# First half-blocks of an attention and FFN kernel: three exponentials for a pair of heads instead of four, and four instructions in another place

## The chip, the cores and the metric

The kernel runs on one core of a Trainium2 chip. Five engines work side by side, each through its own instruction list in order: TensorE (PE in the profile, its weight loads PEld), VectorE (DVE), ScalarE (ACT), GpSimd (POOL) and SyncE (SP). They wait for each other by semaphores only. Transfers from and to HBM are issued from the queues of POOL, SP and ACT and carried by 16 DMA engines. TensorE writes into PSUM, eight banks of 128 partitions x 2 KB; VectorE and ScalarE read PSUM, POOL does not.

The metric is the device time of one execution in microseconds, the median of several runs.

## The reference

Inputs are q, k, v of shape (4, 8, 768, 64) in float32 (batch, heads, sequence, head size) and the weights of an FFN of 512 to 2048 to 512. An attention in which each query sees only the six best chunks of 32 keys is followed by an FFN with a squared relu.

```python
k_min, k_max = k_chunks.min(3), k_chunks.max(3)          # (B, H, 24, 64)
ub = sum(maximum(q * k_min, q * k_max), -1)              # upper bound per query and chunk
ub = where(causal, ub, -1e9)
top_chunks = argsort(ub)[..., -6:]
scores = q @ k.T / 8
scores = where(selected_chunk & causal, scores, -1e9)
attn = softmax(scores)
x = (attn @ v) as (B * S, H * D)                         # (3072, 512)
h = maximum(x @ w_in, 0)
out = (h * h) @ w_out
```

## The kernel before

The work is cut into half-blocks of 384 queries (three tiles of 128): `ORDER` lists (batch, half) as (0,0), (1,0), (0,1), (1,1), (2,0) and so on. Each half-block has four slots, one for each pair of heads; slot s of the first group (s = 0 to 3, `s < NP`) is pair s of batch 0, half 0. The order of instructions is written out by hand: a loop over the first four slots, then a loop over the others, in which FFN steps of earlier half-blocks are put between attention steps from a `queue`.

Steps of a slot, by name and line:

- `step_T` (L267, L274): TensorE transposes the packed keys and queries of a slot into PSUM. In the first loop, keys of slot s+2 go to the pool psF (two banks, shared with FFN blocks), queries to psY (one bank).
- `relus_T` (L295, ScalarE): relu of the queries and of their negative, for the bounds.
- `extrema` (L237, L240, VectorE): minimum and maximum of each chunk of keys, and their block form. Parts 0, 1 and 2 can be placed apart.
- `place` (L300): copies transposed keys or queries to where the scores read them, one copy for each head; by ScalarE or VectorE, as the call says.
- `step_U` (L378, L382, L396, L398): bounds of all chunks by TensorE, the eight largest by VectorE, and a compare that marks the chunks not selected.
- `step_V` (L431, L436 in the first group; L442, L447 later): transposes the marks (in the first group with the queries) and copies them next to the queries. The scores of the slot need this copy. The marks enter the scores as 32 more rows of the contraction.
- `step_E(s, hh, n)` (L460, L468, L471): scores of head hh for PSUM bank n, and their exponential by ScalarE into `e`. In a half 0, a head has six causal blocks of 128x128: `BANKS[0]` puts four of them (keys of tiles 0 and 2) into a first bank of 512 columns, and two (keys of tile 1) into columns 256 to 511 of a second one. In the first group the causal triangle is added in PSUM by one more matmul for each diagonal block (L468, `tri`); from slot 4 on POOL zeroes it after the exponential (L475).
- `step_F` (L493, L502, L503): probabilities times v, division by the sum, into `x`.
- `x_T`, `x_copy` (L531, L537): for the first half-block, x is transposed by TensorE in two parts (pairs 0 and 1, pairs 2 and 3), and copied out of PSUM as one [128x768] copy each.
- `ffn_up` (L579, L585, L589, L590): one of 16 blocks of the hidden layer, with relu on ScalarE and square on VectorE; `ffn_down` (L602): a quarter of an output tile. `push(0)` queues the first half-block's FFN in slot 4.

The end of slot 3 leads over to slot 4: x's first part is copied by ScalarE, then ScalarE places slot 4's queries and half of its keys, and in slot 4 (`if s == NP`) slot 5 is transposed, x's second part copied by VectorE, slot 4's head 0 computed and slot 5's queries placed by ScalarE.

In slot s of the first loop the order is: head 0's first bank, keys of s+2 transposed, head 0's second bank, head 1's first bank, bounds of s+1, three filler matmuls (`busy`), head 1's second bank, queries of s+2 transposed, marks of s+1 transposed, `step_F(s-1)`.

Loads are issued by POOL from lists by slot (`at(s, ...)`, `go`). The FFN's first matrix comes in three transfers (512, 512 and 1024 of its 2048 columns), the second in two. Each POOL transfer uses one of eight semaphores in turn, so an issue waits until the transfer eight before it has landed.

Of the kernel before, what the change touches and what calls it, by code (L numbers as in the profile page):

```python
# [8 lines left out]
F32 = mybir.dt.float32  # L9
BF16 = mybir.dt.bfloat16  # L10
AX = mybir.AxisListType
ALU = mybir.AluOpType
ACT = mybir.ActivationFunctionType
# [9 lines left out]
BANKS = (  # L23
# [3 lines left out]
)  # L27
# [12 lines left out]
def kernel(  # L40
# [9 lines left out]
    nc = tc.nc  # L50
# [3 lines left out]
    NP = H // 2  # L54
# [4 lines left out]
    scale = 1.0 / (D ** 0.5)  # L59

    consts = ctx.enter_context(tc.tile_pool(name="consts", bufs=1))
    work = ctx.enter_context(tc.tile_pool(name="work", bufs=2))
    psS = ctx.enter_context(tc.tile_pool(name="psS", bufs=3, space=bass.MemoryType.PSUM))
# [8 lines left out]
    KR = D + CR  # L72

    kqs = [consts.tile([128, NP, 4, 2, HB], BF16, tag=f"kq{i}", name="kq") for i in range(2)]
# [75 lines left out]
    ident = consts.tile([128, 128], BF16, tag="ident")  # L150
    make_identity(nc, ident)

    tri = consts.tile([128, 128], BF16, tag="tri", name="tri")
# [64 lines left out]
    def col_of(half, j, i):  # L218
        for n, bank in enumerate(BANKS[half]):
            for (at, jj, i0, m) in bank:  # L220
                if jj == j and i0 <= i < i0 + m:
                    return 512 * n + at + 128 * (i - i0)
        raise KeyError

    slots = [(b, half, p) for b, half in ORDER for p in range(NP)]
    NS = len(slots)
    st = {}
# [16 lines left out]
    def in_order(x):  # L244

        return x.rearrange("r (j p) -> r p j", j=TP)

    def by_token(x):
        return x.rearrange("r (p j) -> r p j", j=TP)
# [36 lines left out]
    def relus_T(s):  # L286
        b, half, p = slots[s]
        t = st[s]
        qr = t["qr"] = work.tile([128, 2, HB], BF16, tag="qr", bufs=3, name="qr")
        c = 128 * (1 - half)  # L290
        for w in range(2):
            o, i = qr[:, w, c:], t["q"][:, c:]
            if s >= NP:
                o, i = by_token(o), in_order(t["q"])[:, c // TP:, :]
            nc.scalar.activation(o, i, ACT.Relu, scale=(-1.0, 1.0)[w])  # L295

    def place(s, n, copy, h0=0, h1=2):
        b, half, p = slots[s]
        for h in range(h0, h1):
            copy(by_token(kqs[b % 2][0:D, p, 2 * half + "kq".index(n), h, :]),  # L300
                 in_order(st[s][n][D * h:D * h + D]))
# [103 lines left out]
    def qc(s, h):  # L405
        b, half, p = slots[s]
        return kqs[b % 2][0:KR, p, 2 * half + 1, h, :]
# [16 lines left out]
    def step_V(s):  # L424
# [21 lines left out]
        for h in range(2):  # L446
            nc.vector.tensor_copy(  # L447
                kqs[b % 2][D:KR, p, 2 * half + 1, h, c:], qt[CR * h:CR * h + CR, c:])

    def step_E(s, hh, n):  # L450
        b, half, p = slots[s]
        t = st[s]
        if n == 0:
            t["e"][hh] = work.tile([128, 1920], BF16, tag="e", bufs=4, name="e")
        e = t["e"][hh]
        ps = psS.tile([128, 512], F32, tag="ps", name="ps")
        lo, hi = 512, 0
        for (at, j, i0, m) in BANKS[half][n]:
            c = 128 * (i0 - HT * half)
            nc.tensor.matmul(  # L460
                ps[:, at:at + 128 * m],
                lhsT=kqs[b % 2][0:KR, p, 2 * (j // HT), hh,
                                128 * (j % HT):128 * (j % HT + 1)],
                rhs=qc(s, hh)[:, c:c + 128 * m], start=s >= NP or lo == 512, stop=s >= NP)
            lo, hi = min(lo, at), max(hi, at + 128 * m)
        if s < NP:
            for (at, j, i0, m) in BANKS[half][n]:
                nc.tensor.matmul(  # L468
                    ps[:, at:at + 128], lhsT=ident, rhs=tri, start=False,
                    stop=at == BANKS[half][n][-1][0])  # L470
        nc.scalar.activation(e[:, 512 * n + lo:512 * n + hi], ps[:, lo:hi], ACT.Exp,  # L471
                             scale=float(scale))
        if n == 1 and s >= NP:
            d = e[:, 0:1152].rearrange("p (a c) -> p a c", a=3)[:, :, 0:128]
            nc.gpsimd.affine_select(  # L475
                out=d, in_=d, compare_op=ALU.is_ge, fill=0.0, base=0,
                channel_multiplier=-1, pattern=[[0, 3], [1, 128]])
# [5 lines left out]
    def step_F(s, hh):  # L483
        b, half, p = slots[s]
        t = st[s]
        if hh == 0:
            t["po"] = psA.tile([128, 2, HT, D + 1], F32, tag="att", name="po")
        po = t["po"]
        for i in range(HT):
            iq = HT * half + i  # L490
            for j in range(iq + 1):
                c = col_of(half, j, iq)
                nc.tensor.matmul(  # L493
                    po[:, hh, i, :], lhsT=t["e"][hh][:, c:c + 128],
                    rhs=vn[b % 2][:, 2 * p + hh, j, :],
                    start=(j == 0), stop=(j == iq))
        if hh == 1:
            if p == 0:
                xs[s // NP] = work.tile([128, NP, HT, 128], BF16, tag="x", name="x")
            x = xs[s // NP]  # L500
            r = work.tile([128, 2, HT, 1], F32, tag="r", name="r")
            nc.vector.reciprocal(r, po[:, :, :, D:D + 1])  # L502
            nc.vector.tensor_mul(  # L503
                x[:, p].rearrange("p j (h d) -> p h j d", h=2),
                po[:, :, :, 0:D], r.to_broadcast([128, 2, HT, D]))
            if s // NP and s < NS - 1 and s != 2 * NP - 1:
                nc.sync.dma_start_transpose(
                    out=xT_of(s // NP)[:, p, :].rearrange("r (j t) -> r j t", j=HT),
                    in_=x[:, p].rearrange("p j t -> p (j t)"))
            st.pop(s)  # L510
# [7 lines left out]
    def xT_of(hb):  # L518
        if hb not in xTs:
            xTs[hb] = late.tile([128, NKI, HB], BF16, tag="xT", name="xT")  # L520
        return xTs[hb]
# [14 lines left out]
    def x_copy(hb, g, u0, u1, copy):  # L536
        copy(xT_of(hb)[:, 2 * g + u0:2 * g + u1, :], pts[hb, g][:, u0:u1, :])  # L537
# [89 lines left out]
    def at(s, fn, *a):  # L627
        later.setdefault(s, []).append(lambda: fn(*a))
# [13 lines left out]
    at(0, load_w_in, 512, 1024)  # L642
    for j in range(HT):
        at(1, load_vt, 1, j)
    at(1, load_w_in, 1024, 2048)
    for n in "kq":
        at(2, load_packed, n, 2, 0, H // 2)
        at(5, load_packed, n, 2, H // 2)
# [27 lines left out]
    def go(s, n):  # L676
        for _ in range(n):
            if later.get(s):
                later[s].pop(0)()

    def busy(n, pool=psA, tag="att"):

        idle = pool.tile([128, 128], F32, tag=tag, name="idle")
        for _ in range(n):
            nc.tensor.matmul(idle, lhsT=ident, rhs=ident, start=True, stop=True)  # L685
# [21 lines left out]
    step_cast("q", 1)  # L707
    step_V(0)
    step_T(1, F, Y, "k")
    step_E(0, 0, 0)  # L710
    step_T(1, F, Y, "q")
    relus_T(1)
    step_E(0, 0, 1)
    extrema(1)
    step_T(2, F, Y, "k")
    extrema(2, 0)
# [2 lines left out]
    for s in range(NP):  # L719
        last = s + 1 == NP  # L720
        if s:
            step_E(s, 0, 0)
            if not last:

                step_T(s + 2, F, Y, "k")
                extrema(s + 2, 0)
            step_E(s, 0, 1)
        if last:
            step_F(s - 1, 0)
            step_F(s - 1, 1)  # L730
        step_E(s, 1, 0)
        step_U(s + 1)
        if not last:
            busy(3)
            extrema(s + 2, 1)
            place(s + 1, "k", nc.scalar.copy)
        step_E(s, 1, 1)
        if last:
            x_T(0, 0, F)
            x_copy(0, 0, 0, 2, nc.scalar.copy)  # L740
            place(s + 1, "q", nc.scalar.copy)
            place(s + 1, "k", nc.scalar.copy, 1, 2)
            step_F(s, 0)
            step_F(s, 1)
            step_V(s + 1)
        else:
            step_T(s + 2, F, Y, "q")
            relus_T(s + 2)
            step_V(s + 1)
            if s:  # L750
                step_F(s - 1, 0)
                step_F(s - 1, 1)
            extrema(s + 2, 2)
            if s + 2 == NP:
                place(s + 2, "k", nc.vector.tensor_copy, 0, 1)
        go(s, 99)
# [6 lines left out]
    for s, (b, half, p) in enumerate(slots):  # L763
# [16 lines left out]
        if s == NP:  # L780
            step_P(s + 1)
            x_T(0, 1, F)
            x_copy(0, 1, 0, 2, nc.vector.tensor_copy)
            relus_T(s + 1)
            for n in range(hf):
                step_E(s, 0, n)
            push(0)
            extrema(s + 1)
            place(s + 1, "k", nc.vector.tensor_copy)
            place(s + 1, "q", nc.scalar.copy)  # L790
        if s == 2 * NP:
            for n in range(hf):
                step_E(s, 0, n)
# [146 lines left out]
```

## Time and profile before

| | us |
|---|---|
| median of three runs | 265.12 |
| lowest and highest | 264.89, 265.48 |
| the profiled execution | 265.17 |
| its span in the profile | 263.5 |

| engine | busy us | share of the span | instructions |
|---|---|---|---|
| PE | 253.6 | 96% | 2398 |
| PEld | 157.4 | 60% | 2424 |
| DVE | 162.9 | 62% | 619 |
| ACT | 178.4 | 68% | 399 |
| POOL | 91.0 | 35% | 134 |

The time of an execution is its span and 1.7 us around it. The page's rows of slices cut the span into 40 equal parts of 6.6 us; a digit is the busy share in tenths. In timelines a row is: start in the span, length from the first start to the last end, engine, line, operation, output and inputs with their sizes, and the count of merged instructions; brackets hold idle time of the engine before it and what ended it. Instructions of one engine overlap at their ends, so the time that one holds its engine is the distance from its start to the next one's start.

### The profile page before, as it was taken

How to read it: one execution, taken by the hardware profiler on the slowest of the kernel's cores; microseconds unless marked ns; L12 is line 12 of the kernel's file. 1: busy time of each engine (PE TensorE's matmuls, PEld its weight loads, DVE VectorE, ACT ScalarE, POOL GpSimd, SP SyncE). 2: the span in 40 equal slices, each digit the busy share in tenths (PEclk: the TensorE clock that was granted, in tenths of full speed). 3: DMA queues.
4: the chain of work that ended last, by engine and by line, in shares of the span. 5: the costliest groups of instructions: out<-in, count | busy, mean ns of one | idle time of the engine just before them, and what ended most of it. 6: DMA issues, size and time to landing. Idle time of an engine off the chain costs nothing.

```text
span 263.5 us, 6549 instructions
## 1 busy us (share of the span) xinstructions
PE 253.6 (96%) x2398; PEld 157.4 (60%) x2424; DVE 162.9 (62%) x619; ACT 178.4 (68%) x399; POOL 91.0 (35%) x134
## 2 busy tenths in 40 slices
PE   7898899999999999999999999999999999999995
PEld 6576565556676566655565566745565665645543
DVE  6788998867995568566875566554863233424411
ACT  4899997698984787944785778835685788614500
POOL 8957445607911444225520552310221111000000
PEclk9999999999999999999999999999999999999999
DMA  7999999999994999999995999995642220111022
GB/s 138 166 188 188 207 219 183 131 196 137 135 154 96 138 163 165 142 152 150 189 133 138 142 145 145 166 165 131 112 110 62 67 45 17 56 42 41 0 82 80
DMA packets 116162, 33.69 MB, mean 128 GB/s; under 512 B 102561, under 2 KB 112577, under 8 KB 116129
## 3 DMA queue, kind: packets, MB, share of 16 engines
q0 software_dynamic: 65200, 13.83, 64.0%
q1 hardware_dynamic: 49984, 19.03, 38.2%
q10 hardware_dynamic: 944, 0.39, 0.6%
q8 instruction: 19, 0.31, 0.5%
q14 instruction: 15, 0.11, 0.2%
HBM read 27.26 MB, written 6.29 MB: 127 GB/s over the span
## 4 chain that ended last, share of the span: by engine, by line
PE 88%; ACT 5%; DVE 4%; issue 2%; POOL 0%; ACTq 0%; POOLq 0%
PE ph L579 29%; PE py L602 29%; PE ps L460 13%; PE po L493 8%; ACT e L471 2%; PE ub L382 2%; PE idle L685 2%; PE py L567 1%; PE tk L274 1%; ACT kq L300 1%; DVE km L343 1%; PE qt L431 1%; DVE km L237 1%; PE qt L442 1%; ACT qr L295 1%
## 5 line engine op out<-in xcount | busy, mean ns | idle before, releaser
L471 ACT ACTIVATE e<-ps 128x512 bf16<-128x512 f32 x192 | 96.8, 550 | 18.6 <-PE ps L460 16.9
L579 PE MATMUL ph<-xT,w_in 128*128 128x384 bf16 x512 | 98.9, 325 | 0.7 <-ACT h L585 0.5
L602 PE MATMUL py<-w_out,h 128*128 128x512 bf16 x342 | 82.7, 379 | 1.9 <-issue 0.3
L590 DVE TENSOR_TENSOR h<-ht 128x384 bf16<-128x384 bf16 x114 | 41.8, 376 | 55.4 <-ACT ht L589 54.9
L475 POOL TENSOR_SCALAR_AFFINE_SELECT e<-e 128x384 bf16<-128x384 bf16 x56 | 30.1, 537 | 127.6 <-ACT e L471 127.5
L589 ACT ACTIVATE ht<-ph 128x384 bf16<-128x384 f32 x114 | 55.5, 500 | 26.9 <-PE ph L579 26.5
L579 PEld LDWEIGHTS <-w_in 128*128 128x128 bf16 x512 | 47.9, 97 | 31.4 <-issue 2.1
L460 PE MATMUL ps<-kq 96*128 96x384 bf16 (+2 forms) x320 | 58.0, 278 | 1.4 <-DVE kq L436 1.2
L602 PEld LDWEIGHTS <-h 128*128 128x128 bf16 x368 | 34.7, 97 | 35.3 <-issue 0.6
L460 PEld LDWEIGHTS <-kq 96*128 96x128 bf16 x320 | 26.4, 97 | 16.1 <-issue 1.7
L493 PEld LDWEIGHTS <-e 128*128 128x128 bf16 x672 | 25.2, 98 | 3.9
L493 PE MATMUL po<-vn,e 128*128 128x65 bf16 x672 | 26.8, 194 | 0.0
L396 DVE MAX8 m<-ub 128x8 f32<-128x16 f32 (+4 forms) x160 | 16.2, 168 | 15.7 <-PE ub L389 9.3
L608 ACT COPY ob<-py 128x512 f32<-128x512 f32 x18 | 10.6, 586 | 22.6 <-PE py L602 22.3
L503 DVE TENSOR_TENSOR x<-po,r 128x384 bf16<-128x384 f32 x32 | 17.8, 558 | 1.1
L109 POOL DMA_DIRECT2D kn<-in_k_dram x15 | 13.4, 897 | 0.4 <-issue 0.3
L237 DVE TENSOR_REDUCE km<-tk 128x12 bf16<-128x384 bf16 x24 | 12.5, 551 | 1.5 <-PE tk L274 1.2
L109 POOL DMA_DIRECT2D qn<-in_q_dram x15 | 13.3, 895 | 0.2
L125 POOL DMA_DIRECT2D vn<-in_v_dram x15 | 12.5, 842 | 2.3 <-DMA qn<-in_q_dram 1.5
L343 DVE TENSOR_TENSOR km<-km 128x384 bf16<-128x384 bf16 (+3 forms) x40 | 12.0, 300 | 1.1
L382 PEld LDWEIGHTS <-qr 128*128 128x128 bf16 x160 | 7.8, 96 | 4.1 <-DVE qr L323 1.0
L382 PE MATMUL ub<-kbd,qr 128*128 128x48 bf16 (+1 forms) x160 | 9.6, 180 | 0.6 <-DVE kbd L240 0.3
(79 smaller groups left out, 193.3 us busy)
## 6 DMA issues: line engine op xcount, KB each, us to landing
out_dram<-ob SPq DMA_DIRECT2D x23, 256.0 KB, 2.5
w_out<-in_moe_w_out_dram POOLq DMA_DIRECT2D x2, 1024.0 KB, 18.0
kn<-in_k_dram POOLq DMA_DIRECT2D x15, 128.0 KB, 6.0
qn<-in_q_dram POOLq DMA_DIRECT2D x15, 128.0 KB, 5.8
kq<-kqT SPq DMA_DIRECT2D x10, 192.0 KB, 4.7
vn<-in_v_dram POOLq DMA_DIRECT2D x4, 384.0 KB, 8.1
vn<-in_v_dram POOLq DMA_DIRECT2D x9, 128.0 KB, 8.0
w_in<-in_moe_w_in_dram POOLq DMA_DIRECT2D x2, 512.0 KB, 9.2
```

Of the source, the lines that this page charges most:

```text
L109: nc.gpsimd.dma_start(out=nat_of(n, g)[:, DM * j:DM * j + DM].rearrange("p (h d) -> p h d", d=D), in_=rows(n, *ORDER[g], 0, H)[:, 128 * j: ...
L382: nc.tensor.matmul(ub[:, j - j0], lhsT=st[s]["qr"][:, w, 128 * j:128 * (j + 1)], rhs=kbds[b % 2][:, p, w, :, 0:ncs], start=bool(half) and ...
L396: nc.vector.max(out=m8[:, j, hh, :], in_=ub[:, j - j0, hh, 0:12 * half + 4 * j + 4])
L460: nc.tensor.matmul(ps[:, at:at + 128 * m], lhsT=kqs[b % 2][0:KR, p, 2 * (j // HT), hh, 128 * (j % HT):128 * (j % HT + 1)], rhs=qc(s, hh)[: ...
L471: nc.scalar.activation(e[:, 512 * n + lo:512 * n + hi], ps[:, lo:hi], ACT.Exp, scale=float(scale))
L475: nc.gpsimd.affine_select(out=d, in_=d, compare_op=ALU.is_ge, fill=0.0, base=0, channel_multiplier=-1, pattern=[[0, 3], [1, 128]])
L493: nc.tensor.matmul(po[:, hh, i, :], lhsT=t["e"][hh][:, c:c + 128], rhs=vn[b % 2][:, 2 * p + hh, j, :], start=(j == 0), stop=(j == iq))
L503: nc.vector.tensor_mul(x[:, p].rearrange("p j (h d) -> p h j d", h=2), po[:, :, :, 0:D], r.to_broadcast([128, 2, HT, D]))
L579: nc.tensor.matmul(ph[:, 0:HB], lhsT=w_in[:, ki, 128 * f:128 * (f + 1)], rhs=xT[:, ki, :], start=(ki == 0), stop=(ki == NKI - 1))
L589: nc.scalar.activation(ht, ph[:, 0:HB], ACT.Relu)
L590: nc.vector.tensor_mul(h, ht, ht)
L602: nc.tensor.matmul(py[t], lhsT=h2[hb, f][:, 128 * t:128 * (t + 1)], rhs=w_out[:, f, :], start=(f == 0), stop=(f == NFI - 1))
```

## The change

- `first_E` replaces `step_E` for slots 0 to 3. The two first banks (one for each head) stay as they were, each with its exponential over 512 columns. The two second banks become one bank, 256 columns for each head, with one exponential over 512 columns. Both heads' probabilities lie in one `e` tile; `step_F` computes the columns accordingly. The order of the three banks is head 0's first, head 1's first, the shared one. The count of matmuls stays.
- In slots 1 and 2 the keys of slot s+2 are transposed, and their minima taken, ahead of the slot's first scores instead of behind them. Head 0's second bank, which stood ahead of the bounds of the next slot, is now part of the bank behind them.
- x's first copy goes from ScalarE to VectorE.
- In slot 4 the queries of slot 5 are placed ahead of the scores of slot 4's head 0 instead of behind them, on ScalarE as before.
- The last 1024 columns of w_in are loaded in two transfers of 512.

```diff
+    def first_E(s, n):
+
+        b, half, p = slots[s]
+        t = st[s]
+        if n == 0:
+            t["e"][0] = t["e"][1] = work.tile([128, 1920], BF16, tag="e", bufs=4, name="e")
+        ps = psS.tile([128, 512], F32, tag="ps", name="ps")
+        tiles = ([(n, *x) for x in BANKS[half][0]] if n < 2 else
+                 [(hh, 256 * hh, 1, 1, 2) for hh in range(2)])
+        for i, (hh, at, j, i0, m) in enumerate(tiles):
+            nc.tensor.matmul(
+                ps[:, at:at + 128 * m],
+                lhsT=kqs[b % 2][0:KR, p, 0, hh, 128 * j:128 * (j + 1)],
+                rhs=qc(s, hh)[:, 128 * i0:128 * (i0 + m)], start=i == 0, stop=False)
+        for i, (hh, at, j, i0, m) in enumerate(tiles):
+            nc.tensor.matmul(
+                ps[:, at:at + 128], lhsT=ident, rhs=tri, start=False, stop=i == 1)
+        nc.scalar.activation(t["e"][0][:, 512 * n:512 * n + 512], ps, ACT.Exp,
+                             scale=float(scale))
...
@@ step_F
                 c = col_of(half, j, iq)
+                if s < NP:
+                    c = 512 * hh + c if c < 512 else 256 + 256 * hh + c
...
-    at(1, load_w_in, 1024, 2048)
+    at(1, load_w_in, 1024, 1536)
+    at(1, load_w_in, 1536, 2048)
...
     step_T(1, F, Y, "k")
-    step_E(0, 0, 0)
+    first_E(0, 0)
     step_T(1, F, Y, "q")
     relus_T(1)
-    step_E(0, 0, 1)
     extrema(1)
...
         if s:
-            step_E(s, 0, 0)
             if not last:
 
                 step_T(s + 2, F, Y, "k")
                 extrema(s + 2, 0)
-            step_E(s, 0, 1)
+            first_E(s, 0)
         if last:
             step_F(s - 1, 0)
             step_F(s - 1, 1)
-        step_E(s, 1, 0)
+        first_E(s, 1)
         step_U(s + 1)
         if not last:
             busy(3)
             extrema(s + 2, 1)
             place(s + 1, "k", nc.scalar.copy)
-        step_E(s, 1, 1)
+        first_E(s, 2)
         if last:
             x_T(0, 0, F)
-            x_copy(0, 0, 0, 2, nc.scalar.copy)
+            x_copy(0, 0, 0, 2, nc.vector.tensor_copy)
             place(s + 1, "q", nc.scalar.copy)
...
             relus_T(s + 1)
+            place(s + 1, "q", nc.scalar.copy)
             for n in range(hf):
                 step_E(s, 0, n)
             push(0)
             extrema(s + 1)
             place(s + 1, "k", nc.vector.tensor_copy)
-            place(s + 1, "q", nc.scalar.copy)
```

What is left out of the diff is the removal from `step_E` of what only slots 0 to 3 used.

More of the change, by code (lines that the diff above doesn't have):

```diff
@@ L463, in step_E @@
                                 128 * (j % HT):128 * (j % HT + 1)],
-                rhs=qc(s, hh)[:, c:c + 128 * m], start=s >= NP or lo == 512, stop=s >= NP)
+                rhs=qc(s, hh)[:, c:c + 128 * m], start=True, stop=True)
             lo, hi = min(lo, at), max(hi, at + 128 * m)
[L466 to L470, printed above, removed]
         nc.scalar.activation(e[:, 512 * n + lo:512 * n + hi], ps[:, lo:hi], ACT.Exp,
                              scale=float(scale))
-        if n == 1 and s >= NP:
+        if n == 1:
             d = e[:, 0:1152].rearrange("p (a c) -> p a c", a=3)[:, :, 0:128]
```

## The prediction

> **What bounds the kernel now.** I read the page first, then its slices, then windows cut at the slot borders of the first group of four slots, then the chain of waits, and last the timeline of each engine.
>
> ```profile
> span 263.5 us, 6549 instructions
> ...
> PE   7898899999999999999999999999999999999995
> ...
> ACT  4899997698984787944785778835685788614500
> ```
>
> TensorE is the bound for most of the span, but its row has an 8 in the second, fourth and fifth slice (6.6 us each), and there ScalarE stands at 8 to 9. Windows by stage say more (PE, PEld, DVE, ACT and POOL busy, then clock, DMA share, GB/s):
>
> ```profile
> 13.33:16.76 3.43, 3.16 (x57) 2.40 (x57) 2.79 (x11) 3.27 (x8) 1.31 (x2) 1.00 1.72 189
> 16.76:20.14 3.38, 3.11 (x59) 2.53 (x56) 2.94 (x13) 3.27 (x9) 2.35 (x3) 1.00 1.21 189
> 20.14:26.38 6.24, 5.25 (x83) 3.85 (x81) 5.06 (x19) 5.74 (x14) 4.42 (x7) 1.00 1.70 188
> 26.92:44.00 17.08, 16.68 (x183) 10.61 (x184) 15.99 (x57) 15.57 (x39) 9.78 (x14) 1.00 1.25 209
> ```
>
> The first three rows are slots 1 to 3, the third with the handover to slot 4. ScalarE is the fullest engine in each (3.27 of 3.38, 5.74 of 6.24). From 26.92 on TensorE is full: 16.68 of 17.08. So the head ends where TensorE gets its third FFN block, at 26.92, and what that comes sooner, the end comes sooner, if nothing later stalls. The chain of waits (start, length) agrees: it runs over ScalarE from 16.76 to 26.92 with one short visit to TensorE.
>
> ```profile
> 16.76 1.51 ACT e L471 x3
> ...
> 21.89 0.69 ACT xT L537
> ...
> 24.56 0.35 issue
> ...
> 26.92 1.46 PE ph L579 x8
> ```
>
> ScalarE's own timeline (start, length; a row's start to the next row's start is what an instruction holds the engine, since ends overlap):
>
> ```profile
> 13.33 1.51 ACT L471 ACTIVATE e<-ps 128x512 bf16<-128x512 f32 x3 [0.19 <-PE ps L468]
> ...
> 17.67 0.60 ACT L471 ACTIVATE e<-ps 128x512 bf16<-128x512 f32 x1
> ...
> 18.16 0.96 ACT L300 COPY kq<-tk 64x384 bf16<-64x384 bf16 x2
> 19.15 0.38 ACT L471 ACTIVATE e<-ps 128x256 bf16<-128x256 f32 x1
> 19.43 0.66 ACT L295 ACTIVATE qr<-tq 128x256 bf16<-128x256 bf16 x2
> 20.14 1.75 ACT L471 ACTIVATE e<-ps 128x512 bf16<-128x512 f32 x4
> 21.77 0.81 ACT L537 COPY xT<-pt 128x768 bf16<-128x768 bf16 x1
> 22.45 0.97 ACT L300 COPY kq<-tq 64x384 bf16<-64x384 bf16 x2
> ...
> 23.88 0.66 ACT L295 ACTIVATE qr<-tq 128x256 bf16<-128x256 bf16 x2
> 24.91 0.60 ACT L471 ACTIVATE e<-ps 128x512 bf16<-128x512 f32 x1 [0.37 <-ACT qr L295]
> 25.41 0.95 ACT L300 COPY kq<-tq 64x384 bf16<-64x384 bf16 x2
> 26.38 0.87 ACT L585 ACTIVATE h<-ph 128x384 bf16<-128x384 f32 x2
> ```
>
> **One exponential and keys ahead: slots 1 and 2.** Slot 2 holds ScalarE from 16.76 to 20.14: a 512 and a 256 to 17.67 (0.91), a 512 to 18.16 (0.49), two key copies to 19.15 (0.99), a 256 to 19.43 (0.28), two relus with a wait to 20.14 (0.71): 3.38. After: three 512s (1.48), the copies (0.97 without the gap), two relus at 0.27 each: 2.99. The drop from four exponentials to three is 1.68 less 1.48, 0.20; the other 0.19 is waits, and they go only if TensorE and VectorE turn the slot round in under 3.0 too. That is what the moved transposes decide:
>
> ```profile
> 16.17 0.38 PE L460 MATMUL ps<-kq 96*128 96x384 bf16 x2 [0.27 <-DVE kq L436]
> 16.39 0.28 PE L468 MATMUL ps<-tri,ident 128*128 128x128 bf16 x2
> 16.59 0.37 PE L274 MATMUL tk<-ident,kn 96*64 96x96 bf16 x8
> 16.90 0.28 PE L460 MATMUL ps<-kq 96*128 96x256 bf16 x1
> ```
>
> TensorE waits for the copy of the queries (line 436, on VectorE), then does head 0's first scores, key transposes (16.59 to 16.90, 0.31), head 0's second bank (about 0.17: it is 128 columns of scores less and one mask less than the 0.33 that a first bank takes up to the next), head 1's first bank, the bounds. After, the transposes run while that copy runs, and the second banks come behind the bounds; so the bounds, and with them the selection and the next copy, come 0.31+0.17 = 0.48 sooner after a copy. If this loop alone set the 3.38 before, it would now take 2.90. VectorE is busy 2.94 of the slot's 3.38 (second window) with the same list as after. So ScalarE's 2.99 is the longest of three near limits; I take 3.0. From the first exponential of slot 1 to that of slot 3 it was 20.14-13.33 = 6.81, and becomes 6.0: **0.81**. If the loop keeps the lead, less (first rival). Slot 0 gains nothing: its bounds wait for relus behind the first exponential, and those stay where they are.
>
> **Slot 3 and x's copy.** From 20.14 to the query copies at 22.45 ScalarE spends 2.31, of which 0.68 is x's copy (21.77 to 22.45). After, from 13.33+6.0 = 19.33: a 512 to 19.83, a wait, two more 512s (0.99). The wait is new: slot 3's second score block stands behind step_F(2), which reads the second half of v:
>
> ```profile
> 9.72 2.28 POOL L125 DMA_DIRECT2D vn<-in_v_dram  x3
> DMA to landing us min/median/max: 7.9/8.4/8.7
> ...
> 20.05 0.53 PE L493 MATMUL po<-vn,e 128*128 128x65 bf16 x12
> ```
>
> The last of the three is issued at about 11.2 and lands 7.9 later, at 19.1. It was 0.9 early for 20.05; step_F(2) would now start at 19.1, take 0.4 (0.53 less the last matmul's flight) and the block 0.50 (16.17 to 16.39+0.28): the exponential starts at 20.04 instead of 19.83, 0.21 of wait. Sum 1.70 against 2.31: **0.61**. step_F(3) now needs the shared exponential, which ends at 20.04+0.49+0.60 = 21.1, so its result comes at 21.7; before, VectorE got it at 22.28 (below). The copy goes to VectorE, where the same shape stands, with idle time before it and near it:
>
> ```profile
> 22.28 0.20 DVE L502 RECIPROCAL r<-po 128x6 f32<-128x6 f32 x1 [0.30 <-PE po L493]
> 24.38 0.56 DVE L537 COPY xT<-pt 128x768 bf16<-128x768 bf16 x1 [0.68 <-ACT qr L295]
> 24.85 1.01 DVE L237 TENSOR_REDUCE km<-tk 128x12 bf16<-128x384 bf16 x2
> ```
>
> It holds VectorE 0.47 (24.38 to 24.85), from about 21.2, after the compare of slot 4's bounds; behind it are the reciprocal and product of x's last quarter, which get their input at 21.7 anyway. From there: 0.8 for both, 0.4 for the transposes, 0.6 for the second copy, 0.5 for the rest of the first FFN block, at 24.1, and ScalarE takes that block at 24.5 to 24.7 (below): 0.4 of cover. Without it the copy costs up to 0.47. The Trainium skill, "VectorE: DVE Perf Modes", section Specifications, says that VectorE sits closer to SBUF and ScalarE closer to PSUM, against moving a copy out of PSUM to VectorE. The trace differs: this copy took 0.56 there and 0.81 on ScalarE; by the rule the cover would be thinner and the sum the same.
>
> **Queries placed sooner.** Before: two relus from 23.88, exponential only at 24.91 after 0.37 idle (0.35 of it "issue": nothing that the profile shows), copies 25.41, first relu of the FFN 26.38: 2.50. After: relus 0.54, copies 0.97, exponential 0.50, FFN: 2.01. So 0.49 if the unexplained 0.35 doesn't come again, 0.14 if it does; I take **0.35**, nearer the first, since the exponential now stands behind copies and its scores wait for nothing. Behind it all FFN evictions wait, sooner by the sum.
>
> **The split load.** w_in's last quarters become two transfers: 0.8 more issue on POOL, and each issue behind it waits for the transfer eight before it, one later than before. What this could make late is w_out's second half:
>
> ```profile
> 20.41 0.77 POOL L631 DMA_DIRECT2D w_in<-in_moe_w_in_dram  x1
> DMA to landing us min/median/max: 11.6/11.6/11.6
> ...
> 26.92 0.90 POOL L636 DMA_DIRECT2D w_out<-in_moe_w_out_dram x1 [0.73 <-DMA vn<-in_v_dram]
> DMA to landing us min/median/max: 16.6/18.0/19.4
> ...
> 48.78 2.54 PE py L602 x11
> ...
> 27.00:29.00 2.00, 2.00 (x14) 1.14 (x13) 1.95 (x9) 1.60 (x5) 1.36 (x2) 1.00 1.12 215
> 34.00:36.00 2.00, 2.00 (x27) 1.17 (x26) 1.87 (x8) 1.73 (x5) 0.08 (x2) 1.00 1.25 208
> ```
>
> It lands at 26.92+19.4 = 46.3 (the last two-transfer row's maximum); the seventeenth py matmul is its first reader, 48.78+3x0.215 = 49.43, so 47.7 after the change. Lines of the undivided w_in moved at 215 GB/s (27 to 29), w_out's lines, as long as the halves' will be, at 208: 1 MB takes 0.16 longer. Bounds: nothing below; above, 1.4, where it begins to cost. I take 0. The Trainium skill, "DMA: Bandwidth & Descriptors", section Anatomy of one DMA, gives each such transfer a fixed 2.0 us. If that were paid in the queue, the landing would be 48.3 and the stall 0.6, a time of 264.0; the trace shows transfers of this queue overlapping, and I give it 3 in 100.
>
> **Sum.** 0.81+0.61+0.35 = 1.77. The profiled execution took 265.17 (span 263.5, 1.7 around it), 0.05 over the median of 265.12. 265.17-1.77 = 263.4. After the handover TensorE has the same work and 0.4 idle in 17, so I carry the gain to the end whole.
>
> **Rivals.**
> - The loop of TensorE and VectorE, not ScalarE, keeps the lead in slots 1 and 2, so that only the exponential's 0.20 a slot is saved: 0.40+0.61 and nothing in slot 4: 264.1. For it: TensorE is busy 3.11 of 3.38. Against: 0.48 of that leaves the loop.
> - Handed back later: VectorE is busy 15.99 of 17.08 after 26.92, so slots 4 to 7 might be paced by it and by transfers, not by what precedes them: about 265.1. Against: all its inputs come sooner too, and it has 1.1 idle.
> - Slower: POOL's order. If w_out's second half had to wait for the first of the split loads (issued at 20.41; the whole landed 11.6 later, at 32.0, and its second half is 2.4 of that at 215 GB/s, so 29.6) and then took its 19.4, it would land at 49.0 to 49.9 with the split's cost; TensorE, in order, stops at 47.7 for up to 2.2: 265.6. It is slower than before from a landing after 49.4 on. Against: counting eight back from it in the new order gives the third part of a v load, issued just ahead of 20.41.
> - More: no wait at step_F(2) and no unexplained gap: 0.81+0.82+0.49 = 2.12, 263.0.
>
> **How the numbers follow.** The forecast 0.61, the slow loop 0.16, more 0.07, the page's fixed cost 0.03, handed back 0.05, slower by POOL's order 0.05, and 0.03 for a slowdown I can't name. A measurement of this kernel can tell 0.2%, 0.5 us. Faster 0.87, same 0.05, slower 0.08. The forecast's own range is 263.1 to 263.8; with the slow loop and the larger gain the range is 262.9 to 264.3.
>
> **What would show it.** In the profile after: slots 1 and 2 about 3.0 long between first exponentials; idle time before scores for the copy (line 436's) down, with key transposes inside it; a wait of TensorE for v's transfer near 19.1; x's first copy on VectorE at 21.2; the first FFN relu at 24.5 and the third FFN block at 25.0 to 25.3 instead of 26.92; no wait for w_out near 47.7. Wrong would be cycles of 3.2 or more with VectorE ending ScalarE's waits, or the FFN sooner at 25 but TensorE idle between 25 and 60.

## The result, and the profile after

| | us |
|---|---|
| before, median of six runs | 265.31 |
| after, median of six runs | 264.09 (263.33 to 264.47) |
| ratio, 95% interval | 0.9955, 0.994 to 0.997 |
| profiled executions, before and after | 265.17 and 264.47 |
| their spans | 263.5 and 262.8 |

Faster, by 1.2 at the median; 0.7 in the profiled execution, the slowest of its six. 263.4 was forecast. The 264.09 lies inside the 262.9 to 264.3 that the prediction gave with its slow loop and its larger gain, and above the 263.1 to 263.8 of the forecast itself. The head became nearly as much shorter as forecast, and a part of that was lost again behind it. First the page and the windows (columns as before), cut at the first exponentials of slots 1 to 3, at the first FFN relu and from the third FFN block on:

```profile
span 262.8 us, 6543 instructions
...
PE   7899998999999999999999999999999999999995
...
ACT  4899887698884778934685778836685788614500
```

```profile
13.35:16.32 2.97, 2.97 (x55) 2.50 (x54) 2.35 (x11) 2.94 (x8) 1.65 (x3) 1.00 1.73 177
16.32:19.51 3.19, 2.67 (x50) 2.15 (x48) 2.63 (x11) 3.06 (x8) 1.77 (x3) 1.00 1.37 183
19.51:24.72 5.21, 4.83 (x75) 3.57 (x72) 4.94 (x18) 4.87 (x11) 3.71 (x5) 1.00 1.63 188
25.25:44.00 18.75, 17.26 (x193) 10.75 (x192) 17.69 (x63) 16.21 (x40) 11.89 (x17) 1.00 1.29 206
```

The slots of 3.43, 3.38 and 6.24 are 2.97, 3.19 and 5.21 long. The last row is what the forecast didn't have: TensorE idles 1.5 of 18.75, where it idled 0.4 of 17.08 before. ScalarE's timeline shows the head step by step:

```profile
13.35 1.09 ACT L467 ACTIVATE e<-ps 128x512 bf16<-128x512 f32 x2 [0.26 <-PE ps L465]
...
16.32 1.10 ACT L467 ACTIVATE e<-ps 128x512 bf16<-128x512 f32 x2
...
19.51 0.60 ACT L467 ACTIVATE e<-ps 128x512 bf16<-128x512 f32 x1
20.26 1.08 ACT L467 ACTIVATE e<-ps 128x512 bf16<-128x512 f32 x2 [0.15 <-PE ps L465]
21.23 0.95 ACT L300 COPY kq<-tq 64x384 bf16<-64x384 bf16 x2
...
23.25 0.95 ACT L300 COPY kq<-tq 64x384 bf16<-64x384 bf16 x2
24.23 0.60 ACT L486 ACTIVATE e<-ps 128x512 bf16<-128x512 f32 x1
24.72 0.95 ACT L602 ACTIVATE h<-ph 128x384 bf16<-128x384 f32 x2
```

Slot 3's second exponential waits (0.75 behind the first, where 0.49 is the step of two in a row); the queries stand ahead of slot 4's exponential, and the gap of 0.35 "issue" didn't come again. The same stretch, and what follows, on TensorE:

```profile
15.32 0.37 PE L274 MATMUL tk<-ident,kn 96*64 96x96 bf16 x8
15.62 0.39 PE L460 MATMUL ps<-kq 96*128 96x384 bf16 x2
...
17.50 0.37 PE L274 MATMUL tq<-ident,qn 96*64 96x96 bf16 x8 [0.25 <-DMA qn<-in_q_dram]
...
19.31 0.58 PE L510 MATMUL po<-vn,e 128*128 128x65 bf16 x12
19.73 0.38 PE L460 MATMUL ps<-kq 96*128 96x384 bf16 x2
...
25.25 0.97 PE L596 MATMUL ph<-xT,w_in 128*128 128x384 bf16 x5
...
36.48 0.25 PE L382 MATMUL ub<-kbd,qr 128*128 128x24 bf16 x4 [0.39 <-DVE kbd L240]
...
42.51 0.36 PE L510 MATMUL po<-vn,e 128*128 128x65 bf16 x6 [0.68 <-POOL e L490]
```

Keys are transposed ahead of the scores (15.32, then 15.62). At 17.50 TensorE waits for a transfer that the slower slots of before had covered: slot 4's queries. The third FFN block starts at 25.25 instead of 26.92. Then come two waits that before didn't have, or not at this size: 0.39 at the bounds that are computed in slot 6 (those of slot 7), where before waited 0.16, and 0.68 for POOL.

```profile
37.85 0.25 PE L382 MATMUL ub<-kbd,qr 128*128 128x24 bf16 x4 [0.16 <-DVE kbd L240]
```

POOL's timeline gives the reason for the 0.68, first after, then before:

```profile
25.24 0.89 POOL L653 DMA_DIRECT2D w_out<-in_moe_w_out_dram  x1 [1.92 <-DMA w_in<-in_moe_w_in_dram]
...
33.52 0.53 POOL L490 TENSOR_SCALAR_AFFINE_SELECT e<-e 128x384 bf16<-128x384 bf16 x1
...
37.67 0.71 POOL L490 TENSOR_SCALAR_AFFINE_SELECT e<-e 128x384 bf16<-128x384 bf16 x1 [0.66 <-ACT e L486]
41.01 0.89 POOL L125 DMA_DIRECT2D vn<-in_v_dram  x1 [2.63 <-DMA w_out<-in_moe_w_out_dram]
41.91 0.54 POOL L490 TENSOR_SCALAR_AFFINE_SELECT e<-e 128x384 bf16<-128x384 bf16 x1
```

```profile
39.73 0.89 POOL L125 DMA_DIRECT2D vn<-in_v_dram  x1
41.30 0.51 POOL L475 TENSOR_SCALAR_AFFINE_SELECT e<-e 128x384 bf16<-128x384 bf16 x1 [0.67 <-ACT e L471]
```

A v load may only be issued when the transfer eight before it, w_out's first half, has landed (40.72). That landing is set by the queue and didn't come sooner with the head: it was at 39.10 before, at 39.44 in unsplit (after without the split load, below), and behind the split load it is later still. Slot 6's masking (line 490, POOL's zeroing of the causal triangle) stands behind the load, so TensorE's step_F(6) waits. Before, the same load (39.73) waited for nothing and the masking behind it for ScalarE alone. The 0.39 comes from VectorE. One of its squares (line 607, the squaring of an FFN block after its relu) meets the masking of 33.52:

```profile
33.64 0.63 DVE L607 TENSOR_TENSOR h<-ht 128x384 bf16<-128x384 bf16 x1
```

A square takes 0.358 at the median; this one 0.63. VectorE is nearly full there (17.69 of 18.75), and from this square to the block form of the keys at 36.24, for which these bounds wait, its instructions follow one another, so what it loses reaches them.

The lead over before, read at the start of the n-th weight load of the FFN's first product (four to a block, so the thirteenth opens the fourth block; expectations that say "block" beyond the fourth count these loads), says where the time went. All kernels of the study stand in one table:

```
load                 13     25     33     49     65    481   profiled us
start before      27.41  30.94  33.28  37.93  56.77  242.73  265.17
after              1.66   1.66   1.60   1.37   0.70   0.70   264.47
late_v             1.80   1.66   1.51   1.22   0.89   0.91   264.25
late_v_q           2.01   1.96   1.81   1.52   1.18   1.19   264.00
unsplit            1.64   1.61   1.35   1.36   1.36   1.38   263.81
split_only        -0.31  -0.31  -0.31  -0.31  -0.31  -0.30   265.48
no_mask_5to7       2.00   1.88   1.73   1.73   1.81   1.80   263.37
by_heads           2.16   1.52   1.37   1.29   1.28   1.27   263.91
keys_after         1.34   1.34   1.29   1.28  -0.90  -0.89   266.07
own_banks          1.65   1.65   1.57   1.57   0.74   0.39   264.80
x_scalar           1.44   1.44   1.38   1.38   1.38   1.38   263.80
w_out_later        2.31   2.31   2.25   2.25   2.11   2.12   263.06
w_out_unread       1.97   1.97   1.91   1.91   1.90   1.91   263.27
w_out_half         2.01   2.01   1.95   1.95   1.95   1.96   263.21
```

Each row is one execution. After gains 1.66 by the handover and hands 0.96 back between 31 and 57 us: 0.23 between loads 33 and 49, where TensorE waits 0.39 at the bounds in slot 6, and 0.67 between loads 49 and 65, where it waits 0.68 for POOL.

### The profile page after: what moved, and what is told of

Read it like the earlier page. It is cut to its first block, busy times and chain, and to the rows that moved or that the text cites. A ratio compares the mean times of both kernels' runs of the same rounds, so it can differ in the third digit from the quotient of the medians.

```text
span 262.8 us, 6543 instructions
## 1 busy us (share of the span) xinstructions
PE 253.2 (96%) x2398; PEld 157.8 (60%) x2424; DVE 162.7 (62%) x620; ACT 177.0 (67%) x394; POOL 91.9 (35%) x135
## 4 chain that ended last, share of the span: by engine, by line
PE 83%; DMA 6%; DVE 4%; issue 3%; ACT 2%; POOL 1%; DVEq 0%; POOLq 0%; ACTq 0%
PE py L619 29%; PE ph L596 29%; PE ps L480 12%; PE po L510 7%; DMA qn<-in_q_dram 3%; DMA kn<-in_k_dram 3%; PE ub L382 1%; PE py L584 1%; DVE km L343 1%; ACT ht L606 1%; ACT e L486 1%; DVE x L520 1%; PE qt L442 1%; PE tk L274 1%; PE tq L274 1%
## 5 line engine op out<-in xcount | busy, mean ns | idle before, releaser
L486 ACT ACTIVATE e<-ps 128x512 bf16<-128x512 f32 (+2 forms) x176 | 89.4, 555 | 17.8 <-PE ps L480 17.6
L480 PE MATMUL ps<-kq 96*128 96x384 bf16 (+2 forms) x296 | 53.0, 278 | 0.0
L480 PEld LDWEIGHTS <-kq 96*128 96x128 bf16 x296 | 24.3, 97 | 14.2 <-DVE kq L447 0.4
```

The source lines that it names most:

```text
L480: nc.tensor.matmul(ps[:, at:at + 128 * m], lhsT=kqs[b % 2][0:KR, p, 2 * (j // HT), hh, 128 * (j % HT):128 * (j % HT + 1)], rhs=qc(s, hh)[: ...
```

## The experiments

**Where the 0.96 goes: POOL's order.** late_v takes the third v load of slot 6 out from ahead of the masking; late_v_q moves a query load of slot 5 as well.

```diff
 # late_v
-        at(6, load_vt, 0, HT + j)
+        at(6 + j // 2, load_vt, 0, HT + j)
 # late_v_q: also
-        at(5, load_packed, n, 2, H // 2)
+        at(5 if n == "k" else 6, load_packed, n, 2, H // 2)
```

> The changed kernel with one move: the last of the three transfers of batch 0's second v half goes from slot 6 to slot 7, behind slot 6's last masking by POOL. Theory (the head's gain of 1.67 is lost again where POOL waits for w_out's first half to land and the masking of slot 6 stands behind that wait): the wait of TensorE for POOL before step_F(6), 0.68, is gone, the FFN blocks stay 1.35 ahead of before, and the time is about 0.6 below the changed kernel's: 263.4 to 263.6. Rival (slots 4 to 7 are paced by VectorE and ScalarE, and POOL's lateness only shows it): another wait takes its place, within 0.2 of the changed kernel's 264.1.

> As the run with v's last transfer later, and also the second half of the third query group's load goes from slot 5 to slot 6, so that POOL doesn't wait for the second of the split loads ahead of slot 5's maskings. Theory: besides the 0.68 also the 0.23 lost at slot 6's bounds comes back (VectorE's square beside POOL's masking takes 0.35 instead of 0.63); the blocks stay 1.6 ahead of before to the end, 263.1 to 263.4. Rival (the 0.23 is pacing by VectorE): no better than the run with v alone.

Medians 263.66 (ratio 0.995, 0.993 to 0.9969) and 263.45 (0.9939, 0.9917 to 0.996). In late_v the wait for POOL is gone from TensorE's waits (columns: engine and line, what it waited for, us in total, times, longest), but another stands in its place:

```profile
PE ub L382 <- DVE kbd L240: 0.8, 2, 0.4
...
PE qt L442 <- DVE chosen L398: 0.4, 1, 0.4
```

Behind it is a square again, as VectorE's and POOL's timelines of late_v show:

```profile
32.78 0.68 DVE L607 TENSOR_TENSOR h<-ht 128x384 bf16<-128x384 bf16 x1
...
37.53 0.95 DVE L607 TENSOR_TENSOR h<-ht 128x384 bf16<-128x384 bf16 x2
```

```profile
32.64 0.67 POOL L104 DMA_DIRECT2D qn<-in_q_dram  x1 [2.47 <-DMA w_in<-in_moe_w_in_dram]
...
37.76 0.52 POOL L490 TENSOR_SCALAR_AFFINE_SELECT e<-e 128x384 bf16<-128x384 bf16 x1 [0.66 <-ACT e L486]
```

Two squares that hold VectorE 0.61 elsewhere took 0.95. The square at 32.78, ahead of the bounds in slot 6, took 0.68; beside it POOL was issuing a query load until 33.31. So the v load was the cause of the 0.68, but with it gone 0.91 of 1.80 still went, where after lost 0.96 of 1.66. The rival in the expectation, another wait in its place, was right. late_v_q kept 1.18 of 2.01 (in its execution slot 4's queries landed early enough for no wait at 17). Neither median parts from after's by its interval.

**Squares beside maskings.** no_mask_5to7 is late_v_q without the causal masking of slots 5 to 7, which it leaves out:

```diff
-        if n == 1:
+        if n == 1 and not NP < s < 2 * NP:
```

> The kernel with later v and q loads, and without POOL's causal masking in slots 5 to 7 (that part of the computation is left out: pairs 1 to 3 of batch 1, half 0 attend to later tokens inside their chunks). Theory (what is still lost between 27 and 42, 0.83 in that run, comes from VectorE's squares that run beside POOL's maskings and take 0.63 to 0.69 instead of 0.35, on a path that VectorE paces): no square over 0.5 there, the FFN blocks stay as far ahead at 42 as at 27, but for 0.2 at slot 5's bounds, and the time is 0.5 to 0.7 lower, 262.8 to 263.0. Rival (VectorE has too much work in slots 5 to 7 whatever POOL does): the same 0.8 is lost and the time stays 263.4.

Median 263.34, ratio 0.9923 (0.991 to 0.9935), the only interval wholly below after's. From load 33 on nothing is lost: 1.73, 1.73, 1.81. Its median is only 0.11 below that of its starting point late_v_q, where 0.5 to 0.7 was expected, and the two intervals overlap: the time alone shows nothing, and what follows rests on the profiles. late_v_q has no wait of TensorE for POOL between 26 and 57, so it isn't the time of the maskings themselves that was saved. Its waits for VectorE from load 33 on, 0.39 at the bounds in slot 6 and 0.42 for the compare behind them, became 0.16 and none. So the collision costs lead, and in after it and POOL's order are the 0.96.

How it works can be read from ends. In after the square at 33.64 ended at 34.27, the masking of 33.52 at 34.05: 0.22 later. In late_v the squares ended at 38.48, the masking at 38.28: 0.20 later. In by_heads (below) a square took 1.22 and ended 0.22 behind the second of two maskings. The fourteen traces have 283 squares that began while a masking ran; all but that one ended 0.20 to 0.30 behind the end of that masking, 0.21 at the median, whether they began early or late in it. So the square is held until the masking ends. Why 0.21 is left then, and not the whole 0.358, the traces don't show. The Trainium skill, "SBUF — State Buffer", section SBUF: two separate sides, says that VectorE instructions with two SBUF inputs and POOL's instructions that read SBUF take a shared pair of ports as an exclusive lock: the one that starts first has it for its whole length, and the other is blocked. The traces agree, in the other direction too: after's masking at 37.67 began 0.02 behind the start of a square and took 0.71 instead of 0.52, while late_v's masking at 37.76 began 0.03 ahead of a square, took 0.52, and held that square for 0.69.

Maskings are not the only cause of long squares. Of 159 squares that met nothing on POOL but the issue of a transfer, 18 took 0.47 to 0.70 and the others no more than 0.42. What in an issue holds a square is open.

**The split load, alone and undone.** split_only is before with the split, unsplit is after without it.

> The kernel before with nothing but the split load. Theory: POOL's later transfers shift, but the compute in front of them is 1.7 later than in the changed kernel, so the masking of slot 6 is about 0.7 late for POOL's own order and just in time for step_F(6): 0 to 0.3 slower than before, 265.3 to 265.6. If the split costs by itself what the changed kernel lost: 1.0 slower, 266.3.

> The changed kernel with w_in's last 1024 columns in one transfer as before. Theory (the lane that POOL waits for is the matter, and without the split w_out's first half is issued when the first part of w_in has landed, near 22.4 instead of 25.2, and lands 1 to 1.5 sooner): no wait of TensorE for POOL before step_F(6). But the ninth FFN block, now at 31.7, needs the whole transfer, which landed at 32.0 before and 32.4 here: TensorE stops there for 0.6 to 0.9. Together 263.8 to 264.3, no clear difference from the changed kernel. If the split is only a cost and the block doesn't wait: 263.4.

split_only: 265.22, ratio 0.9999 (0.9989 to 1.0009): nothing, as the prediction had it. unsplit: 263.75, ratio 0.9958 (0.9942 to 0.9974): no difference from after at the end, but another inside. Its first half of w_out is issued sooner (22.45 instead of 25.24), so the v load of slot 6 is issued at 39.73 (after: 41.01), TensorE waits for no masking, and 1.38 of 1.64 stay. The stall of 0.6 to 0.9 at the ninth block, expected from w_in landing whole, was about 0.1: it landed at 31.89 and released its reader at 31.93, 0.62 behind the first weight load of the step_F ahead of it, where after has 0.51.

**The head's parts, one undone at a time.** by_heads is late_v_q with slot 4 to 7's first loads cut by heads, so that no transfer is late in the head; the other three are by_heads with one part of the change undone, each run in one execution only.

```diff
 # by_heads
-        load_packed(n, 1)
+        load_packed(n, 1, 0, H // 2)
 ...
+    for n in "kq":
+        load_packed(n, 1, H // 2)
 # keys_after: first_E(s, 0) ahead of step_T(s + 2, "k"), extrema(s + 2, 0)
 # own_banks: first_E(s, 2) and first_E(s, 3), 256 columns and one exponential each
 # x_scalar
-            x_copy(0, 0, 0, 2, nc.vector.tensor_copy)
+            x_copy(0, 0, 0, 2, nc.scalar.copy)
```

> The kernel with later v and q loads, and the loads of the second key and query group cut by heads: heads 0 to 3, then v's second half, then heads 4 to 7. Theory (the head's gain varies by the landing of those queries, 16.96 to 17.49 in four profiles against TensorE's need at 17.2, and of v against 19.1): both land about 1.5 sooner, no wait for a transfer before 27, and the third FFN block comes 2.0 to 2.2 ahead of before in any execution; 263.2 to 263.4 and a spread under 1. Rival (the wait at 20.04 that I put down to v is TensorE's or VectorE's own pace): handover ahead by 1.8 as without it, no lower time.

> by_heads with one part undone: in slots 1 and 2 the key transposes stand behind the first score block again, inside the loop of query copy, scores, bounds, selection. The other parts stay. Measure: the lead over the kernel before at the weight load of the fourth FFN block (the 13th w_in load: 27.41 before, 25.25 in by_heads, lead 2.16). Theory (the prediction's: the transposes' 0.31 leaves the loop in two slots, and the loop is near the limit): the first exponentials of slots 2 and 3 come 0.15 to 0.3 later each than in by_heads (16.14 and 19.13), lead 1.6 to 1.85. Rival (ScalarE alone sets these slots, the transposes' place is worth nothing): same cycles within 0.1, lead 2.05 to 2.2.

> by_heads with one part undone: the second banks of the two heads go through two exponentials of 256 columns (each with its own score tile) in slots 0 to 3, behind the bounds as the shared one does; keys ahead stay. Measure: lead over the kernel before at the 13th w_in load (2.16 in by_heads). Theory (ScalarE is the longest of three near limits; four exponentials hold it 0.20 more a slot, slots 1 to 3): cycles of slots 1 and 2 at 3.15 to 3.2 instead of 2.98, lead 1.5 to 1.8. Rival (the loop of TensorE and VectorE sets the cycles, ScalarE has room): cycles unchanged within 0.05, and only slot 3's 0.2 is lost, lead 1.9 to 2.0.

> by_heads with one part undone: x's first copy is ScalarE's again. Measure: lead over the kernel before at the 13th w_in load (2.16 in by_heads). Theory (it holds ScalarE 0.68 in the chain, and on VectorE it is covered): lead 1.45 to 1.65. Rival (what ends last at the handover is VectorE's second copy of x and not ScalarE, so that ScalarE has part of the 0.68 free): lead 1.8 to 2.1.

The first exponential of slot 1 starts between 13.0 and 13.6 from execution to execution, so I read from it on, on ScalarE's timelines. Slots 1, 2 and 3 of by_heads, of keys_after and of own_banks:

```profile
13.17 1.08 ACT L469 ACTIVATE e<-ps 128x512 bf16<-128x512 f32 x2 [0.26 <-PE ps L467]
...
16.14 1.11 ACT L469 ACTIVATE e<-ps 128x512 bf16<-128x512 f32 x2
...
19.13 1.67 ACT L469 ACTIVATE e<-ps 128x512 bf16<-128x512 f32 x3
...
24.19 0.99 ACT L604 ACTIVATE h<-ph 128x384 bf16<-128x384 f32 x2
```

```profile
13.36 1.33 ACT L469 ACTIVATE e<-ps 128x512 bf16<-128x512 f32 x2 [0.25 <-PE ps L467]
...
16.59 1.30 ACT L469 ACTIVATE e<-ps 128x512 bf16<-128x512 f32 x2
...
19.83 1.79 ACT L469 ACTIVATE e<-ps 128x512 bf16<-128x512 f32 x3
...
25.00 1.00 ACT L604 ACTIVATE h<-ph 128x384 bf16<-128x384 f32 x2
```

```profile
13.55 1.08 ACT L471 ACTIVATE e<-ps 128x512 bf16<-128x512 f32 x2 [0.20 <-PE ps L467]
...
16.56 1.12 ACT L471 ACTIVATE e<-ps 128x512 bf16<-128x512 f32 x2
...
19.60 1.76 ACT L471 ACTIVATE e<-ps 128x512 bf16<-128x512 f32 x4
...
24.73 0.94 ACT L606 ACTIVATE h<-ph 128x384 bf16<-128x384 f32 x2
```

To the first FFN relu it is 11.02 in by_heads (13.05 before). Without keys ahead 11.64, so they are worth 0.62, of which 0.51 in slots 1 and 2 (3.23 and 3.24 instead of 2.97 and 2.99). Without the shared exponential 11.18: worth 0.16, of it only 0.04 and 0.05 in slots 1 and 2 (3.01, 3.04). The rival in its expectation was right: the loop of copy, scores, bounds and selection sets these slots, and ScalarE has room. x_scalar's relu stands at 24.95, 11.71 from its 13.24: the copy is worth 0.69. The lead at load 13 alone, which the expectations name, would mislead: keys_after's 1.34 is 0.26 below the low end of its expectation, and 0.19 of that is that its execution also began 0.19 later than by_heads's.

by_heads gained 2.16 at the handover, as expected, and lost 0.64 of it by load 25. On its POOL both of slot 4's maskings stand behind the issue of w_out's second half, and VectorE's squares meet all three. The first of the pair took 0.67 and ended at 27.69, so it stood beside the issue; the second took 1.22 and stood beside the maskings:

```profile
26.73 0.91 POOL L655 DMA_DIRECT2D w_out<-in_moe_w_out_dram  x1
27.64 1.02 POOL L492 TENSOR_SCALAR_AFFINE_SELECT e<-e 128x384 bf16<-128x384 bf16 x2
```

```profile
27.02 1.86 DVE L609 TENSOR_TENSOR h<-ht 128x384 bf16<-128x384 bf16 x2
```

Its median was 263.57, ratio 0.9937 (0.9922 to 0.9953). The spread, expected under 1, was 1.6 (262.84 to 264.44), which speaks against late transfers in the head as its cause.

**Keeping the lead.** w_out_later is by_heads with that half issued in slot 5.

```diff
-    for g in range(2):
-        at(3 + g, load_w_out, 8 * g, 8 * g + 8)
+    at(3, load_w_out, 0, 8)
...
+    at(5, load_w_out, 8, 16)
     for n in "kq":
         at(2, load_packed, n, 2, 0, H // 2)
```

> by_heads with w_out's second half issued by POOL in slot 5, ahead of that slot's key load, and not in slot 4 ahead of its two maskings. In by_heads those maskings came 1 to 2 late, both beside VectorE's squares, one square took 1.22, and 0.64 of lead was lost between the 21st and 25th FFN block; the lead was 2.16 before it and 1.28 at the end, profiled 263.91 (span 262.2), median 263.57. Theory (a masking that is late meets the squares): no loss there over 0.2, lead at the 25th w_in load 1.95 to 2.15, at the end 1.6 to 1.9, profiled span 261.6 to 261.9, median 262.9 to 263.3. Rival (VectorE is full and the lead is lost to it whatever POOL does, or the half, issued 2 us later, lands late): lead at the end 1.2 to 1.4, median 263.4 to 263.8; a late landing would show as a wait for w_out at 47 to 49.

In its profile the theory held: 2.31, 2.31, 2.25, 2.25, 2.11, 2.12. TensorE idles 0.4 again, as before the change:

```profile
25.10:44.00 18.90, 18.50 (x205) 11.46 (x206) 17.25 (x64) 16.47 (x41) 11.53 (x18) 1.00 1.29 202
```

But 263.06 was the fastest of twelve: the median is 264.18 (263.06 to 266.08), ratio 0.9972 (0.9955 to 0.9989), no better than after and above what theory and rival had. What may have held the others shows in the executions of keys_after and of own_banks, where the queue was slow, in TensorE's waits:

```profile
PE py L621 <- DMA w_out<-in_moe_w_out_dram: 1.0, 1, 1.0
```

```profile
PE py L623 <- DMA w_out<-in_moe_w_out_dram: 0.6, 1, 0.6
```

There the second half landed at 50.3 and 48.7; in the other profiled executions at 45.5 to 47.2, with the same bytes loaded. (keys_after lost 2.18 between loads 49 and 65: this wait of 1.03, one of 0.52 for an exponential and one of 0.40 for POOL make up most of it.) w_out_unread reads the first half in place of the second, and so leaves the second half's part of the product out; w_out_half doesn't load it either.

```diff
 # w_out_unread, in ffn_down; the same index in ffn_last
-                py[t], lhsT=h2[hb, f][:, 128 * t:128 * (t + 1)], rhs=w_out[:, f, :],
+                py[t], lhsT=h2[hb, f][:, 128 * t:128 * (t + 1)], rhs=w_out[:, f % 8, :],
 # w_out_half: also
-    at(5, load_w_out, 8, 16)
```

> w_out_later with every matmul of the second FFN product reading w_out's first half (index f % 8 in place of f); the second half is still loaded in the same place of the same queue, but nothing reads it. So the second half's part of the product is left out (replaced by the first half's numbers), with the same matmuls. w_out_later kept 2.11 of lead in its profiled execution (263.06, half landed at 46.7, no wait), yet its twelve executions spread from 263.06 to 266.08 with median 264.18; in two single looks the half landed at 48.7 and 50.3 and TensorE waited 0.6 and 1.0 for it. Theory (the half's landing changes from execution to execution, and after 2 us of lead TensorE waits for it in most of them): median 263.0 to 263.3, highest at most 264.0. Rival (the spread comes from elsewhere: v, keys or queries behind w_out in the queue, or VectorE beside POOL): median 263.9 to 264.4, highest over 264.8. In between: part of each, and the profile says which transfer TensorE then waits for.

> w_out_unread without the load of w_out's second half at all (2 MB of the 31 us queue are left out, and so is that half's part of the product, as in w_out_unread; the matmuls are the same in number and size). In w_out_unread the highest time fell from 266.08 to 264.25, but the median only from 264.18 to 263.8. Theory (what is left of the spread are transfers: keys, queries and v behind the half land when the queue has worked it off, and POOL's next issue waits for the transfer eight before): median 262.9 to 263.3, highest at most 263.8; lead 1.9 or more from the fourth block to the end in the profile. Rival (the rest is the head's own start, 13.03 to 13.55 for the first exponential in the executions so far, and VectorE beside POOL's masking, which don't care for the queue behind w_out): median 263.6 to 264.0, highest 264.1 or more.

Medians 263.8 (263.27 to 264.25; ratio 0.9953, 0.9939 to 0.9967) and 263.56 (263.21 to 264.34; ratio 0.9948, 0.9931 to 0.9965). Both fall between theory and rival, and neither interval parts from w_out_later's. With the wait for the half taken away no time over 264.34 was left in eleven executions, against four of twelve with it, the highest 266.08; but a spread of 1 remains that neither this wait nor the queue behind it explains. Their profiles (each the fastest execution of its kernel) show no loss. Which wait the other executions have is not settled; a part may be the head's start, 13.03 to 13.55.

## Why the prediction was nearly right, point by point

- **Slots 1 and 2, 0.81.** 6.81 became 6.16 (0.65): the moved transposes did what was worked out, but slot 4's queries landed at 17.46 and held TensorE 0.25, a transfer that the prediction left out. Without that wait (by_heads) it was 5.96, 0.85. The reason was half wrong: I took ScalarE's 2.99 as the longest of three near limits and gave the shared exponential 0.20 a slot. It is worth 0.04; the loop is the limit.
- **Slot 3, 0.61.** 2.31 became 1.72 (0.59). A wait came of the size forecast (0.26 for 0.21), but v was hardly its cause: its last part landed at 19.47, and step_F(2) took 0.42 (19.31 to 19.73) instead of 0.37 in by_heads, where v had landed at 15.5. The rest is step_F(2) itself, on TensorE between the two score blocks. In by_heads the gap is 0.59, since there the first exponential started 0.64 behind its scores and not 0.53. x's copy ran on VectorE here:

```profile
21.48 0.56 DVE L554 COPY xT<-pt 128x768 bf16<-128x768 bf16 x1
```

  It was covered: moving it back cost 0.69 against the 0.68 forecast.
- **Queries sooner, 0.35.** From their first copy at 22.45 to the FFN's relu at 26.38 was 3.93, and is 3.49 (21.23 to 24.72): 0.44, near the upper bound of 0.49. This term was not undone by itself.
- **The head's sum** is thus 1.68 by ScalarE's rows, 1.67 by the third FFN block, for 1.77.
- **The split load at nothing**: right for w_out's reader (it landed at 47.07 and made no wait, so the rival's 48.3 didn't come) and for before. But the later issue of w_out's first half (25.24 instead of 22.49) and its landing (40.72 instead of 39.10) made slot 6's v load wait, and I had followed only w_out's own reader, not the issue that counts eight back to it.
- **"I carry the gain to the end whole"** is the step that failed. 0.96 of 1.66 went between 31 and 57 us in the profiled execution. My rival for it was VectorE's pace, with a chance of 5 in 100 and all of the gain. It was a part of the gain and two mechanisms: POOL's issues bound to the queue's landings, with maskings behind them, and VectorE's squares held by maskings, in late_v also beside an issue. By the medians 265.31-1.68 = 263.6 was to be had, so an execution at 264.09 lost about 0.5, if its head gained as much; that all lose it in these two places is argued from one profile each.
- **The slow loop** as a rival (264.1) gave the time by luck. It had the loop as the limit, rightly, but with nothing gained from keys ahead: 0.40 in slots 1 and 2, where 0.65 was measured, and 1.0 in all, where the head gained 1.7 and lost a part of it later. Its 0.20 a slot for the exponential was 0.04. As it set the upper part of the range, that 264.09 lies inside the range is luck too.

## What to carry to other kernels

When a head gets shorter, ask of every transfer issued in the next stages whether it is bound to the compute or to the queue: what the queue sets does not move, and an engine that issues loads in order carries such a wait to the compute instructions behind it. Cost an added or moved issue by all that stands behind it and by what counts back to it, not by its own reader alone. Undo the parts singly: the part named first in this change (the shared exponential) gave 0.16 of the 2.03 that by_heads gained in the head, the keys' place 0.62 and x's copy 0.69, each read from one execution.

## What was unexpected of the hardware

- A VectorE instruction with two SBUF inputs beside POOL's masking isn't slowed in proportion but held until it ends, and done about 0.21 later: 0.63 to 0.73 instead of 0.36 when it began just behind the masking, and 1.22 when two maskings stood back to back.
- With the same bytes in the same queue, w_out's second half landed at 45.5 to 50.3 in thirteen profiled executions, its issue standing at 26.7 to 28.7. The prediction took one landing as fixed, and its margin of 1.4 is smaller than this spread.
